# Attention decode with a feed-forward layer on one core: values in two contiguous halves, short weight rows over all partitions, a new order of work

## The chip, the cores and the metric

The kernel runs on one core of one Trainium2 chip. The core has a matrix engine (PE, whose weight loads are listed as PEld), a vector engine (DVE), a scalar engine (ACT), GpSimd (POOL) and a queue engine (SP) that issues the transfers from device memory; 16 DMA engines carry them out. The metric is the device time of one execution in microseconds (us), the median of three runs. Three runs of the kernel before took 311.46, 311.53 and 311.90 us.

## The reference

Four tokens (batch 4, sequence 1, width 448) go twice through the same attention layer and the same feed-forward layer. The attention has 16 query heads over 8 key/value heads of width 256, and looks at the last 2,048 of 8,192 cached positions.

```python
W = min(4096, max(256, Sk // 4))                  # 2048
q = (x @ wq) as [B, 16, 1, 256]
k, v = the last W rows of k_cache, v_cache, each head used by two query heads
p = softmax(q k^T * 256 ** -0.5);  o = p v
attention(x) = o @ wo
ffn(x) = (silu(x @ w_gate) * (x @ w_up)) @ w_down  # 448 -> 1792 -> 448

x = x + attention(layernorm(x));  x = x + ffn(layernorm(x))
x = x + attention(layernorm(x));  x = x + ffn(layernorm(x))
```

Both layers read the same caches. Keys and values of one token and one head are 1 MB each (2,048 x 256 in bf16). For 4 tokens and 8 heads that is 67 MB, and the second pass needs it all again. The weights are some 12 MB.

## The kernel before

**Work units.** One unit is a triple of token, layer and key/value head; there are 64. The tuple `PLAN` (line 64) orders them in 32 steps; each string holds groups, and a group is one unit or two joined with `+`. Its steps interleave tokens and layers: token 0 finishes layer 0 at step 4, token 1 at 12, token 2 at 18 and token 3 at 24 (counted from 0). When a token finishes a layer's heads, its output projection, norm and feed-forward and, for layer 0, its next query follow ("the crossing").

**Slots.** Keys and values come as halves of 512 KB into 27 slots of 128 partitions x 4 KB (`half`, line 355, `NPOOL`). `KEEP_K` and `KEEP_V` name how many heads of a token stay in their slots from layer 0 to layer 1; the rest are loaded twice. In all there are 90 key halves and 92 value halves.

**Loads.** A key half (line 817) takes, for each of the 128 partitions, 8 of that partition's 16 consecutive positions: one run of 4,096 bytes. A value half (line 830) takes two of four blocks of 512 positions; in each block a partition has 4 consecutive positions, so it receives two runs of 2,048 bytes. Weights load through `load` (line 495). Rows 384 to 447 of wq, w_gate and w_up are the last 64 of 448. They come as two DMAs each, one for each half of the columns, into partitions 0 to 63 and 64 to 127 (lines 503 and 515). All transfers are issued by SP in one queue.

**One group.** DVE transposes each key half in 32 x 32 blocks of 4-byte words (L822). POOL writes the masked query `qe` (L869). PE makes the scores: 32 matmuls for a group, over 8 slices of the width, two halves, and two parts (`scores1`, L852, for a group of one unit; `scores`, L864, for two). DVE takes maxima (L876, L890), PE spreads them (L881, L884), ACT takes the exponential into `praw` (L895, L898), with gaps between the written elements. PE turns the probabilities so that positions lie on partitions (`turn`, L912): two matmuls over 128 columns add up in the same place, one shifted against the other. ACT copies them out (L920), PE sums them (L928) and multiplies with the values (`pv`, L942, 8 matmuls for each half). DVE, POOL and PE normalise and flip the result (L933, L955, L959, L965, L975), and `out_proj` (L987, L995) adds the head's share of the output projection to a PSUM bank.

**The norm** (line 522) also makes `xe`, the last 64 features placed once in partitions 0 to 63 and once in 64 to 127 with zeros in the other half, as the two weight halves need them: one matmul (L540) and two DVE copies (L543, L545).

**What sets the order.** A planner (`Graph.schedule`, line 176) runs while the program is built. Each operation has an engine, an assumed duration and a rank; the planner walks through assumed time and gives each engine the ready operation of lowest rank. The resulting order is fixed, and each engine runs its list in order, with semaphore waits between engines. A load's rank follows from the unit's place (`KLEAD`, `KTAIL`, `VLAG`) plus an entry of the table `OFF` (line 47), which has 75 entries, for keys and values only. A load takes the slot that is free first. Idle stretches of PE on the assumed time are filled with matmuls on zeros (L1068, L1074). The crossing's operations have a rank 20 places lower than the unit that completes the token (`CROSS`).

The functions that the diff touches, and what calls them:

Of the kernel before, what the change touches and what calls it, by code (L numbers as in the profile page):

```python
# [25 lines left out]
NPOOL = 27  # L26
KEEP_K = (5, 5, 4, 5)
# [20 lines left out]
    ("k", 0, 0, 0): 1, ("k", 0, 0, 1): 2, ("k", 0, 0, 2): 0.5, ("k", 0, 0, 4): -8, ("k", 0, 1, 2): 0.5,  # L48
    ("k", 0, 1, 3): 1, ("k", 0, 1, 4): 4, ("k", 0, 1, 5): -1, ("k", 1, 0, 1): -3, ("k", 1, 0, 2): 1,
    ("k", 1, 0, 3): 1, ("k", 1, 0, 4): 0.5, ("k", 1, 0, 5): 0.5, ("k", 1, 0, 6): 1, ("k", 1, 0, 7): -0.5,  # L50
    ("k", 1, 1, 2): 1.5, ("k", 1, 1, 3): 1, ("k", 1, 1, 4): 1, ("k", 1, 1, 5): 2, ("k", 1, 1, 6): 2,
    ("k", 1, 1, 7): 2, ("k", 2, 0, 2): -1.5, ("k", 2, 0, 3): -2.5, ("k", 2, 0, 4): -2, ("k", 2, 0, 7): -0.5,
    ("k", 2, 1, 1): -2, ("k", 2, 1, 2): -2, ("k", 2, 1, 3): -4, ("k", 2, 1, 4): -2.5, ("k", 2, 1, 6): 2,
    ("k", 3, 0, 1): -0.5, ("k", 3, 0, 3): -0.5, ("k", 3, 0, 4): -2.5, ("k", 3, 0, 5): 1, ("k", 3, 0, 7): -0.5,
    ("k", 3, 1, 0): 1, ("k", 3, 1, 2): -1, ("k", 3, 1, 4): 5.5, ("k", 3, 1, 5): -0.5, ("k", 3, 1, 6): -2,
    ("k", 3, 1, 7): 0.5, ("v", 0, 0, 0): 0.5, ("v", 0, 0, 1): -3, ("v", 0, 0, 3): -3, ("v", 0, 0, 4): -7,
    ("v", 0, 0, 7): -2, ("v", 0, 1, 0): 0.5, ("v", 0, 1, 1): 0.5, ("v", 0, 1, 4): 0.5, ("v", 0, 1, 5): 0.5,
    ("v", 1, 0, 0): -0.5, ("v", 1, 0, 2): -2, ("v", 1, 0, 3): -1, ("v", 1, 0, 6): 1.5, ("v", 1, 1, 0): 1.5,
    ("v", 1, 1, 4): 2, ("v", 1, 1, 5): -1, ("v", 1, 1, 6): -1.5, ("v", 1, 1, 7): 2, ("v", 2, 0, 0): 1.5,
    ("v", 2, 0, 5): 0.5, ("v", 2, 0, 6): -0.5, ("v", 2, 1, 1): 1.5, ("v", 2, 1, 2): 1.5, ("v", 2, 1, 4): 0.5,  # L60
    ("v", 2, 1, 5): 6, ("v", 2, 1, 6): -3, ("v", 3, 0, 0): 2, ("v", 3, 0, 1): 3, ("v", 3, 0, 5): -0.5,
    ("v", 3, 1, 0): -0.5, ("v", 3, 1, 1): -3, ("v", 3, 1, 2): 4, ("v", 3, 1, 4): 2, ("v", 3, 1, 7): -2,
# [35 lines left out]
class Op:  # L98
    __slots__ = ("i", "eng", "dur", "rank", "emit", "deps", "succ", "nbytes", "dsem", "dval",
                 "start", "end", "pos", "waits", "inc", "val", "known", "run", "cell", "rel", "bank")  # L100

    def __init__(self, i, eng, dur, rank, emit):
        self.i, self.eng, self.dur, self.rank, self.emit = i, eng, dur, rank, emit
        self.deps = {}
        self.succ = []
        self.nbytes = 0
        self.dsem = None
        self.dval = 0
        self.cell = None
        self.rel = ()  # L110
        self.bank = ()
        self.inc = False
        self.val = 0
        self.waits = []


class Graph:
    filler = None

# [12 lines left out]
    def op(self, eng, dur, rank, emit, r=(), w=(), bank=(), acc=()):  # L132

        o = Op(len(self.ops), eng, dur, rank, emit)
        o.bank = bank
# [24 lines left out]
    def dma(self, rank, nbytes, emit, sem, r=(), w=(), run=8192, cell=None):  # L160

        o = self.op(SP, 0.05, rank, emit, r=r, w=w)
        o.run = run
        o.nbytes = nbytes
        o.cell = cell
        if cell is None:
            self._count(o, sem)
        return o
# [7 lines left out]
    def schedule(self, npool):  # L176
# [17 lines left out]
        while n < len(self.ops):  # L194
# [16 lines left out]
            if o.cell is not None:  # L211

                slot = min(pool)
                pool.remove(slot)
# [11 lines left out]
            avail[e].remove(o)  # L226
            o.start = t
# [114 lines left out]
def build(nc, A_x, A_k_cache, A_v_cache, A_wq, A_wo, B_x, B_w_gate, B_w_up, B_w_down, out):  # L342
# [3 lines left out]
    with ExitStack() as es:  # L346
# [8 lines left out]
        half = [sb(f"half{s}", [128, 8 * DH], BF16) for s in range(NPOOL)]  # L355
        identb = sb("identb", [128, 128], BF16)
        tiny = sb("tiny", [128, 14 + NS], BF16)
        onesb, qmask, osel, rsel = tiny[:, 0:1], tiny[:, 2:6], tiny[:, 6:10], tiny[:, 10:14]
        pmax = [tiny[:, 14 + s:15 + s] for s in range(NS)]
        tsel = sb("tsel", [128, 4, B], BF16)  # L360
        selt = [sb(f"selt{h}", [128, 4, 12], BF16) for h in range(2)]
        sel1 = [sb(f"sel1{h}", [128, 2, 4, 2, 2], BF16) for h in range(2)]
# [27 lines left out]
        praw = sb("praw", [128, 514], BF16)  # L390
# [28 lines left out]
        def c_fill(e):  # L419
# [7 lines left out]
            e.memset(xe[:, :, :], 0.0)  # L427
# [6 lines left out]
        g.op(DVE, 1.0, R0, c_fill, w=("onesf", "expo", "wrow", "qmask") + XE + XN +  # L434
# [7 lines left out]
        for h in range(2):  # L442
            g.op(DVE, 0.1, R0, lambda e, h=h: e.memset(selt[h][:, :, :], 0.0), w=(f"selt{h}",))
            for P in range(2):
                for y in range(2):
                    c0 = 8 * P + 2 * y
                    g.op(DVE, 0.1, R0, lambda e, h=h, P=P, c0=c0: e.tensor_copy(
                        selt[h][:, :, c0:c0 + 2], ivq[:, 2 * P + h, 0:4, :]), r=("identb",), w=(f"selt{h}",))
# [18 lines left out]
        ivt = identb[:, :].rearrange("p (h x z n) -> p h x z n", h=2, x=2, n=2)  # L467
        for h in range(2):
            for y in range(2):
                for x in range(2):  # L470
                    g.op(DVE, 0.1, R0, lambda e, h=h, y=y, x=x: e.tensor_copy(sel1[h][:, x, :, y, :], ivt[:, h, x, 0:4, :]),
                         r=("identb",), w=(f"sel1{h}{y}{x}",))
        for s_ in range(NS):
# [7 lines left out]
            rmask[:, :], idt.rearrange("p j t -> p t j"), AX.X, ALU.max), r=("identb",), w=("rmask",))  # L481
        iv = identb[:, :].rearrange("p (j z P y n) -> p j z P y n", j=4, P=2, y=2, n=2)
# [12 lines left out]
        def load(rank, nbytes, dst, src, key, run=8192):  # L495
            nw[0] += 1
            g.dma(rank, nbytes, lambda e: e.dma_start(dst, src), f"w{nw[0]}", w=key if isinstance(key, tuple) else (key,), run=run)  # L497

        load(-90, 4000, xio[0:B, :], A_x[:, 0, :], xio_k)
        for cc in range(3):  # L500
            load(-80, 1 << 20, wq_sb[:, 4096 * cc:4096 * (cc + 1)], A_wq[128 * cc:128 * cc + 128, :], f"wq{cc}")
        for h in range(2):
            load(-80, 1 << 18, wq_sb[64 * h:64 * h + 64, 3 * 4096:], A_wq[384:448, 2048 * h:2048 * h + 2048], f"wq3{h}", 4096)
        wo_v = A_wo.rearrange("(k p) n -> p k n", p=128)

        def load_wo(rank, kvh):
            load(rank, 458752, wo_sb[:, 4 * kvh:4 * kvh + 4, :].rearrange("p (h d) n -> p h (d n)", h=2),
                 A_wo[512 * kvh:512 * kvh + 512, :].rearrange("(h p d) n -> p h (d n)", h=2, d=2), f"wo{kvh}", 1792)

        def load_ffn(rank, rank_d):  # L510
            for nm, wsb, src in (("wg", wg_sb, B_w_gate), ("wu", wu_sb, B_w_up)):
                load(rank, 3 * 458752, wsb[:, 0:3 * FF].rearrange("p (c n) -> p c n", c=3),
                     src[0:384, :].rearrange("(c p) n -> p c n", p=128), nm + "a", 3584)
                for h in range(2):
                    load(rank, 114688, wsb[64 * h:64 * h + 64, 3 * FF:], src[384:448, 896 * h:896 * h + 896], f"{nm}b{h}", 1792)
            load(rank_d, 1605632, wd_sb[:, :, :], B_w_down.rearrange("(c p) n -> p c n", p=128), "wd", 896)
# [5 lines left out]
        def norm(t, rank, x):  # L522
# [17 lines left out]
            g.op(PE, 0.06, rank, lambda e: e.matmul(Z2[0:64, 16:17], lhsT=identb[:, 64:128], rhs=xn[:, 3, t:t + 1],  # L540
                                                    start=True, stop=True, skip_group_check=True),
                 r=(f"xn{t}", "identb"), w=("z2",), bank=("Z2",))
            vec(rank, lambda e: e.tensor_copy(xe[64:128, 1, t:t + 1], xn[64:128, 3, t:t + 1]), (f"xn{t}",),  # L543
                (f"xe{t}",), 0.08)
            vec(rank, lambda e: e.tensor_copy(xe[0:64, 0, t:t + 1], Z2[0:64, 16:17]), ("z2",), (f"xe{t}",), 0.1, ("Z2",))  # L545
# [23 lines left out]
        def qproj(ts, rank):  # L569
# [5 lines left out]
            for b, (zb, z, bank) in enumerate(banks):  # L575
# [13 lines left out]
                for c0, c1, rr, kw in ((0, 3, XN, dict(w=(z,))), (3, 4, XE, dict(acc=(z,)))):  # L589
                    g.op(PE, 0.43 * (c1 - c0), rank, lambda e, zb=zb, b=b, c0=c0, c1=c1: q_mm(e, zb, b, c0, c1),  # L590
                         r=rr + tuple(f"wq{c}" for c in ((0, 1, 2) if c0 == 0 else (30, 31))), bank=(bank,), **kw)
# [34 lines left out]
        def ffn_row(ts, rank):  # L626
# [24 lines left out]
            for gi, (z, bank, w) in enumerate((("z", "Z", "wg"), ("z2", "Z2", "wu"))):  # L651
                g.op(PE, 1.28, rank, lambda e, gi=gi: gu(e, gi, 0, 3), r=XN + (w + "a",), w=(z,), bank=(bank,))
                g.op(PE, 0.5, rank, lambda e, gi=gi: gu(e, gi, 3, 4), r=XE + (w + "b0", w + "b1"), acc=(z,), bank=(bank,))
# [491 lines left out]
```

## Time and profile before

| | |
|---|---|
| three runs | 311.46, 311.53, 311.90 us |
| the profiled execution's own time | the page gives its span, 309.8 us, and no other |
| PE, DVE, ACT, POOL busy | 78%, 65%, 23%, 28% of the span |
| read from device memory | 107.58 MB, 347 GB/s over the span |
| hardware DMA queue | 93.3% of the 16 engines' span |
| value halves, key halves | 92 and 90 of 512 KB |
| key transposes on DVE (L822) | 90, 1,234 ns each, 110.5 us in all |

A line of the windows view gives a stretch and its length, the busy time and the number of instructions of each engine, the clock granted to PE, the busy share of the DMA engines (a little over 1 is possible, since packets overlap) and the rate. The chain of waits goes back from the last instruction: at each step to what released it, or to the instruction before it on its engine. SPq is time in SP's queue, "issue" is time in which an engine waited for nothing that the profile shows. The clock is given in parts of full speed.

### The profile page before, as it was taken

What the parts mean: (1) busy time and instruction counts of PE and PEld (TensorE: products, weight loads), DVE (VectorE), ACT (ScalarE), POOL (GpSimd) and SP (SyncE); (2) the same over time, 40 slices, a digit from 0 to 9 for tenths busy, and PEclk for the clock granted to TensorE, in tenths of its full rate; (3) what the DMA queues carried; (4) which work ended last, traced back from release to release, by engine and by line L of the source; (5) the groups of instructions that cost most, each with busy time, mean ns of one, the idle gap of its engine ahead of it and who ended that gap; (6) DMA issues with size and microseconds to landing.
All of it is one profiled execution on the core that took longest, in us unless ns stands there. A gap on an engine that the chain in (4) does not pass through costs nothing.

```text
span 309.8 us, 11390 instructions
## 1 busy us (share of the span) xinstructions
PE 240.2 (78%) x4972; PEld 136.9 (44%) x4972; DVE 202.1 (65%) x641; ACT 70.0 (23%) x203; POOL 88.3 (28%) x233
## 2 busy tenths in 40 slices
PE   0578686776779787799788798788988787986976
PEld 0323224334234444454345545564554446554554
DVE  8534377746254887978587878682689679375542
ACT  0030003131104232313132223211422320231410
POOL 1511102222103233322325332412324322244330
PEclk9999759796577897956787777655857955596975
DMA  7999999999999999999999999999899999899200
GB/s 265 333 383 399 389 403 403 393 394 351 332 394 391 392 394 399 376 381 375 373 369 380 399 397 399 393 395 351 310 382 401 396 393 401 297 324 390 85 3 3
DMA packets 43746, 108.33 MB, mean 350 GB/s; under 512 B 3240, under 2 KB 7344, under 8 KB 43312
## 3 DMA queue, kind: packets, MB, share of 16 engines
q1 hardware_dynamic: 43696, 107.60, 93.3%
q8 instruction: 39, 0.64, 0.9%
q14 instruction: 11, 0.09, 0.1%
HBM read 107.58 MB, written 0.00 MB: 347 GB/s over the span
## 4 chain that ended last, share of the span: by engine, by line
DMA 35%; PE 32%; SPq 15%; DVE 11%; issue 5%; ACT 1%; DVEq 0%
DMA half<-in_A_k_cache_dram 20%; DMA half<-in_A_v_cache_dram 13%; PE Y L942 8%; DVE half L822 6%; SPq L830 5%; SPq L817 5%; PE S L852 5%; SPq L497 4%; PE Z L586 4%; PE Z L702 2%; DVE oh L959 2%; DMA wg_sb<-in_B_w_gate_dram 2%; PE Z L729 2%; PE A L995 1%; PE Z L532 1%
## 5 line engine op out<-in xcount | busy, mean ns | idle before, releaser
L822 DVE STREAM_TRANSPOSE half<-half 128x1024 uint32<-128x1024 uint32 x90 | 110.5, 1234 | 23.6 <-DMA half<-in_A_k_cache_dram 23.3
L955 POOL TENSOR_TENSOR small<-small 128x2 f32<-128x2 f32 (+1 forms) x58 | 42.5, 735 | 81.1 <-DVE small L933 79.4
L942 PE MATMUL Y<-half,pT 128*4 128x256 bf16 (+1 forms) x1024 | 55.1, 324 | 12.2 <-DMA half<-in_A_v_cache_dram 6.9
L852 PE MATMUL S<-half,qe 128*8 128x128 bf16 x1664 | 41.6, 251 | 5.0 <-DVE half L822 2.3
L869 POOL TENSOR_TENSOR qe<-qc,tiny 128x64 bf16<-128x64 bf16 x64 | 18.3, 294 | 77.1 <-PE S L852 47.0
L957 ACT ACTIVATE oh<-Y 128x256 bf16<-128x256 f32 x58 | 22.2, 384 | 72.9 <-PE Y L942 67.5
L898 ACT ACTIVATE praw<-S,small 104x128 bf16<-104x128 f32 x52 | 19.1, 367 | 67.7 <-DVE small L890 67.3
L852 PEld LDWEIGHTS S<-half,qe 128*8 128x8 bf16 x1664 | 29.6, 95 | 10.1 <-DVE half L822 3.8
L959 DVE SCALAR_TENSOR_TENSOR oh<-oh,small,Y 128x256 bf16<-128x256 bf16 x58 | 27.0, 465 | 10.0 <-ACT oh L957 8.9
L942 PEld LDWEIGHTS Y<-half,pT 128*4 128x4 bf16 (+1 forms) x1024 | 20.1, 89 | 24.6 <-DMA half<-in_A_v_cache_dram 12.1
L876 DVE TENSOR_REDUCE tiny<-S 104x1 bf16<-104x128 f32 (+1 forms) x58 | 16.9, 294 | 9.2 <-PE S L852 9.0
L920 ACT ACTIVATE pT<-Y 128x64 bf16<-128x64 f32 (+1 forms) x58 | 13.6, 234 | 27.8 <-PE Y L912 27.5
L1068 PE MATMUL A<-identb,small 128*128 128x512 bf16 x48 | 19.8, 528 | 0.0
L881 PE MATMUL S<-small,identb 104*104 104x32 bf16 x58 | 12.8, 229 | 7.3 <-DVE tiny L876 5.5
L995 PE MATMUL A<-wo_sb,oT 128*4 128x448 bf16 x148 | 15.1, 405 | 2.9 <-DVE oT L975 2.6
L933 DVE TENSOR_REDUCE small<-Y 128x2 f32<-128x32 f32 (+1 forms) x58 | 10.4, 183 | 10.6 <-PE Y L928 10.4
L532 PE MATMUL Z<-st,small 128*128 128x2 f32 x32 | 9.0, 350 | 9.9 <-DVE st L529 9.0
L912 PE MATMUL Y<-sel,praw 104*128 104x32 bf16 x208 | 14.1, 184 | 3.3 <-ACT praw L898 2.8
L965 PE MATMUL Y<-tiny,oh 128*128 128x2 bf16 (+1 forms) x116 | 11.8, 171 | 6.1 <-DVE oh L959 5.3
L975 DVE TENSOR_TENSOR oT<-Y,small 128x4 bf16<-128x4 f32 (+1 forms) x62 | 9.2, 154 | 9.1 <-PE Y L965 8.4
L965 PEld LDWEIGHTS Y<-tiny,oh 128*128 128x128 bf16 x116 | 6.9, 101 | 18.1 <-DVE oh L959 12.9
L586 PE MATMUL Z<-wq_sb,xn 128*4 128x512 bf16 x120 | 14.1, 601 | 0.3 <-DVE st L538 0.3
(137 smaller groups left out, 302.1 us busy)
## 6 DMA issues: line engine op xcount, KB each, us to landing
half<-in_A_v_cache_dram SPq DMA_DIRECT2D x92, 512.0 KB, 9.4
half<-in_A_k_cache_dram SPq DMA_DIRECT2D x90, 512.0 KB, 8.8
wo_sb<-in_A_wo_dram SPq DMA_DIRECT2D x8, 448.0 KB, 13.5
wq_sb<-in_A_wq_dram SPq DMA_DIRECT2D x3, 1024.0 KB, 7.0
wd_sb<-in_B_w_down_dram SPq DMA_DIRECT2D x1, 1568.0 KB, 17.6
wg_sb<-in_B_w_gate_dram SPq DMA_DIRECT2D x1, 1344.0 KB, 15.5
wu_sb<-in_B_w_up_dram SPq DMA_DIRECT2D x1, 1344.0 KB, 16.8
wq_sb<-in_A_wq_dram SPq DMA_DIRECT2D x2, 256.0 KB, 11.6
```

The lines of the kernel that those rows point to most:

```text
L586: last = e.matmul(zb[32 * j:32 * j + B, 0:512], lhsT=lhsT, rhs=wq_sb[:, c:c + 512], start=(cc == 0), stop=(cc == 3), skip_group_check=True)
L822: return e.transpose(a, a)
L852: last = e.matmul(Sb[s_][qd:qd + 8, 0:128], lhsT=qe[q_][:, 0, ce, :, :].rearrange("p a n -> p (a n)"), rhs=kt[:, ce // 2, ce % 2, 2 * x:2 ...
L869: g.op(POOL, 0.25, pos - SLEAD - 1, lambda e, P=P, t=t, kvh=kvh: e.tensor_tensor(qe[q_][:, P, :, :, :], qc[t][:, kvh, :, :].unsqueeze(2).b ...
L898: return e.activation(praw[0:R, 2:258].rearrange("p (g r h l) -> p h g r l", g=2, h=2, l=2)[:, 0, :, :, :], Sb[s_][0:R, 0:128].rearrange(" ...
L942: last = e.matmul(Yb[p_][32 * gg:32 * gg + M, 256:512], lhsT=pT[pt][:, gg, 2 * hv + a, 4 * P:4 * P + M] if n == 2 else p1[:, gg % 2, gg // ...
L955: g.op(POOL, 0.69, pos, lambda e: e.tensor_tensor(ri[p_][:, 0:2 * n], rs[p_][:, 0:2 * n], expo[:, 1:1 + 2 * n], op=ALU.pow), r=(f"rs{p_}", ...
L957: g.op(SCA, 0.34, pos, lambda e: e.activation(oh[:, :], Yb[p_][:, 256:512], ACT.Copy), r=(f"y{p_}",), w=("oh",), bank=(f"Y{p_}",))
L959: g.op(DVE, 0.43, pos, lambda e: e.scalar_tensor_tensor(out=oh[:, :], in0=oh[:, :], scalar=lomask[:, 0:1], in1=Yb[p_][:, 256:512], op0=ALU ...
L965: last = e.matmul(Yb[p_][:, 2 * n * dh:2 * n * dh + 2 * n], lhsT=oh[:, :].rearrange("p (m e) -> p e m", e=2)[:, dh, :], rhs=osel[:, 0:2 * ...
L995: last = e.matmul(Ab[32 * k:32 * k + B, 0:D], lhsT=oT[oi][:, k % 2, k // 2, :], rhs=wo_sb[:, 4 * kvh + k, :], start=False, stop=False, ski ...
L1068: return e.matmul(Ab[:, 0:512], lhsT=zero[:, 0:1].broadcast_to([128, 128]), rhs=identb[:, :].unsqueeze(1).broadcast_to([128, 4, 128]), sta ...
```

## The change

**Values.** The 2,048 positions are cut into two contiguous halves of 1,024. In a half each partition has 8 consecutive positions: one run of 4,096 bytes. With that the positions' places on partitions and in score columns change. A group's score matmul now takes its columns from both key halves at once (`keys`): with one access over two slots, if the slots are at most `REACH` = 15 apart, otherwise with two matmuls of half the width. Whichever of the two key slots is lower holds the first half (`which`). All slots are one tensor for this (`kv`). The planner gives the second key half a free slot near the first (`mate`) and adds 0.35 us to the assumed duration of a pair that is far apart (`FAR_DUR`).

**Turn.** The exponential is written without gaps, and `turn` writes its two results to partitions 0 to 63 and 64 to 127 from 64 columns each, instead of adding two results over 128.

**Last 64 rows.** wq, w_gate and w_up each get one DMA for them: row r goes to partitions 2r and 2r + 1, half of the columns each. `xe` follows: a matmul with `twice` copies each of the 64 features to two partitions, and one DVE multiplication with `par` keeps the right one.

**Order.** `OFF` has 198 entries, for keys (k), values (v), weights (w), groups (g), transposes (t), output projections (o) and crossings (d), and applies to the operations of all engines by a tag. The run lengths that the planner assumes for weights are lower (wq 2000, wo 950, gate and up 800 and 950, down 430).

```diff
 NPOOL = 27
+HALF = 8 * DH
+REACH = 15
+FAR_DUR = 0.35
...
 OFF = {
-    ("k", 0, 0, 0): 1, ("k", 0, 0, 1): 2, ("k", 0, 0, 2): 0.5, ("k", 0, 0, 4): -8, ("k", 0, 1, 2): 0.5,
...
+    ("d", 4): -7, ("d", 12): -6.5, ("d", 18): -7, ("d", 21): 0.5, ("d", 24): -6.5, ("d", 27): -0.5, ("d", 31): 2,
+    ("g", 0, 0, 1): -8, ("g", 0, 0, 3): 4.5, ("g", 0, 0, 4): -7, ("g", 0, 0, 5): -1, ("g", 0, 0, 6): -3,
...
+    ("v", 3, 1, 6): 1.5, ("w", 1): 7, ("w", 2): -8, ("w", 3): 0.5, ("w", 4): 8, ("w", 5): 6, ("w", 7): -4,
...
-        o = Op(len(self.ops), eng, dur, rank, emit)
-        o.bank = bank
+        o = Op(len(self.ops), eng, dur, rank + OFF.get(self.tag, 0.0), emit)
+        o.bank, o.tag = bank, self.tag
...
                 slot = min(pool)
+                if o.mate:
+                    near = [s for s in pool if s[0] <= t + 1e-9 and abs(s[1] - o.mate[0]) <= REACH]
+                    slot = min(near) if near else slot
...
+            o.dur += FAR_DUR * sum(abs(a[0] - b[0]) > REACH for a, b in o.pairs)
...
-        half = [sb(f"half{s}", [128, 8 * DH], BF16) for s in range(NPOOL)]
+        kv = sb("half", [128, NPOOL * HALF], BF16)
...
-        for h in range(2):
-            load(-80, 1 << 18, wq_sb[64 * h:64 * h + 64, 3 * 4096:], A_wq[384:448, 2048 * h:2048 * h + 2048], f"wq3{h}", 4096)
+        load(-80, 1 << 19, wq_sb[:, 3 * 4096:], A_wq[384:448, :].rearrange("r (h c) -> (r h) c", h=2), "wq3", 4096)
...
-                for h in range(2):
-                    load(rank, 114688, wsb[64 * h:64 * h + 64, 3 * FF:], src[384:448, 896 * h:896 * h + 896], f"{nm}b{h}", 1792)
+                load(rank, 229376, wsb[:, 3 * FF:], src[384:448, :].rearrange("r (h c) -> (r h) c", h=2), nm + "b", 950)
...
-            vec(rank, lambda e: e.tensor_copy(xe[64:128, 1, t:t + 1], xn[64:128, 3, t:t + 1]), (f"xn{t}",),
-                (f"xe{t}",), 0.08)
-            vec(rank, lambda e: e.tensor_copy(xe[0:64, 0, t:t + 1], Z2[0:64, 16:17]), ("z2",), (f"xe{t}",), 0.1, ("Z2",))
+            g.op(PE, 0.06, rank, lambda e: e.matmul(Z2[:, 16:17], lhsT=twice[:, :],
+                                                    rhs=xn[:, 3, t:t + 1], start=True, stop=True, skip_group_check=True),
+                 r=(f"xn{t}", "twice"), w=("z2",), bank=("Z2",))
+            vec(rank, lambda e: e.tensor_tensor(xe[:, :, t], par[:, :], Z2[:, 16:17].broadcast_to([128, 2]), op=ALU.mult),
+                ("z2", "par"), (f"xe{t}",), 0.14, ("Z2",))
...
+        def which(cell, kc):
+            return int(cell[0] == max(kc[0][0], kc[1][0]))
+
+        def keys(kc, j, nj, ce):
+            lo, hi = sorted((kc[0][0], kc[1][0]))
+            at = [kv[:, HALF * c + 256 * j + 64 * (ce // 2) + ce % 2:] for c in (lo, hi)]
+            if hi - lo <= REACH:
+                return [(0, bass.AP(at[0].tensor, at[0].offset, [list(at[0].ap[0]), [HALF * (hi - lo), 2], [256, nj], [2, 32]]))]
+            return [(32 * nj * i, bass.AP(v.tensor, v.offset, [list(v.ap[0]), [256, nj], [2, 32]])) for i, v in enumerate(at)]
...
-                    vsrc = A_v_cache[t, kvh, s0:s0 + WIN, :].rearrange("(a q g) d -> q a g d", a=4, q=128)
+                    vsrc = A_v_cache[t, kvh, s0:s0 + WIN, :].rearrange("(a q g) d -> a q (g d)", a=2, q=128)
...
-                            half[cell[0]][:, :].rearrange("p (a g d) -> p a g d", a=2, g=4),
-                            vsrc[:, 2 * hv:2 * hv + 2, :, :]), None, w=(f"v{t}_{kvh}_{hv}",), run=2048, cell=cell)
+                            unit(cell), vsrc[hv]), None, w=(f"v{t}_{kvh}_{hv}",), run=4096, cell=cell)
...
+                    for x in range(X):
                         for P in range(n):
-                            kt = half[kcs[P][hf][0]][:, :].rearrange("p (j c r v) -> p c v j r", j=8, c=4, v=2)
-                            qd = 64 * P + 32 * hf
...
+                            qd = 64 * P + 32 * x
+                            for i, (c0, rhs) in enumerate(keys(kcs[P], J * x, J, ce)):
+                                last = e.matmul(Sb[s_][qd:qd + 8, c0:c0 + rhs.free_size()],
+                                                lhsT=qe[q_][:, P, ce, :, :].rearrange("p a n -> p (a n)"), rhs=rhs,
+                                                start=(ce == 0 and i == 0), stop=(ce == 7), skip_group_check=True)
...
-                        last = e.matmul(o, lhsT=praw[0:R, c0:c0 + 128], rhs=w,
-                                        start=(gg == 0 and h == 0), stop=False, skip_group_check=True)
+                        last = e.matmul(Yb[p_][64 * h:64 * h + 64, c0:c0 + (48 if n == 2 else 32)],
+                                        lhsT=praw[0:R, 64 * gg:64 * gg + 64], rhs=w,
+                                        start=(gg == 0), stop=False, skip_group_check=True)
```

## The prediction

> **What bounds the kernel now.** I read part 2 of the page first: for each fortieth of the span (7.75 us), how busy the 16 DMA engines were and what they moved.
>
> ```profile
> DMA  7999999999999999999999999999899999899200
> GB/s 265 333 383 399 389 403 403 393 394 351 332 394 391 392 394 399 376 381 375 373 369 380 399 397 399 393 395 351 310 382 401 396 393 401 297 324 390 85 3 3
> ```
>
> The engines are full from the second slice to the 37th, about 288 us of 309.8. The rate is not constant: dips at slices 2, 10 to 11, 28 to 29 and 35 to 36, most of them at full occupancy. A shorter transfer stream therefore shortens the kernel, unless the engines behind it cannot follow. Next come windows with something special in them (columns: window, length, PE, PEld, DVE, ACT, POOL, clock, DMA share, GB/s).
>
> ```profile
> 254.00:258.90 4.90, 4.30 (x81) 2.71 (x80) 3.90 (x14) 0.38 (x1) 1.77 (x6) 0.50 1.03 406
> 62.50:66.50 4.00, 2.96 (x79) 1.64 (x79) 1.71 (x8) 0.87 (x3) 1.26 (x3) 1.00 1.05 387
> 10.50:14.00 3.50, 2.50 (x9) 1.79 (x9) 1.27 (x9) 0.00 (x0) 2.89 (x9) 1.00 1.03 245
> 73.00:83.00 10.00, 6.63 (x93) 3.49 (x96) 3.44 (x14) 1.28 (x3) 2.70 (x8) 0.50 1.05 308
> ```
>
> The first holds only keys, the second only values, the third the end of wq's third block and its last rows in two 64-partition loads, the fourth gate and up with theirs. All run at share 1.03 to 1.05; the rate falls to 245 and 308. The packet counts of the first and of the second:
>
> ```profile
> DMA packets 543, 1.99 MB, mean 406 GB/s; under 512 B 60, under 2 KB 60, under 8 KB 542
> ...
> q1 hardware_dynamic: 542, 1.97, 101.3%
> ```
>
> ```profile
> DMA packets 795, 1.55 MB, mean 387 GB/s; under 512 B 47, under 2 KB 47, under 8 KB 794
> ...
> q1 hardware_dynamic: 794, 1.53, 103.7%
> ```
>
> Without the small ones these are 482 packets of 4,096 B and 747 of 2,048 B, so the windows are pure. Keys: 1.97 MB / 4.9 us = 402 GB/s. Values: 1.53 / 4.0 = 382 GB/s. Last, the chain of waits by engine, and its pieces where the last token changes layer:
>
> ```profile
> DMA 35%; PE 32%; SPq 15%; DVE 11%; issue 5%; ACT 1%; DVEq 0%
> ```
>
> ```profile
> 239.97 11.65 DMA half<-in_A_v_cache_dram
> 251.62 0.04 issue
> 251.66 0.60 PE Y L942 x6
> ...
> 256.50 0.15 DVE st L543
> ...
> 273.70 6.91 DMA half<-in_A_k_cache_dram
> 280.60 0.02 issue
> 280.63 0.03 DVE half L822
> ```
>
> DMA and SP's queue are half the chain. Until 251.6 it comes back to a landing; then follow 22 us of token 3's crossing (output projection, norm, feed-forward, next query), a load issued into a freed slot, and compute to 309.8.
>
> **The change part by part.**
>
> *Value runs.* 92 value halves are 48.23 MB. At 382 GB/s they take 126.1 us, at the keys' 402 they take 120.0: 6.1 us less, 0.066 us a half. The new shape, values in one contiguous 512 KB, is not in the trace. Its lower bound is 0 (the rate belongs to the source and not to the run); its upper bound is the 419 GB/s of the windows view from 4.5 to 9.5 us, where wq comes in 8 KB runs: 126.1 - 115.1 = 11.0. I take 6.1, since run and destination are then exactly the keys'. The Trainium skill, "DMA: Bandwidth & Descriptors", section Specifications, gives 512 B as the least transfer for line rate. By that rule 2 KB and 4 KB runs are equal, this term is 0 and the time would be 308.2; the two windows above, 5% apart with full engines, speak against it.
>
> *Last rows of wq.* From 10.5 to 14.0 us the engines move 0.86 MB. At 402 GB/s this takes 2.1 us, so 1.4 is saved. Bounds: 0 (slow for another reason) and 1.4.
>
> *Last rows of gate and up.* 73 to 83 us moves 3.08 MB in 10.0 us. At the 382 GB/s of the stretch 83 to 84 us, which is only w_down's short packets, it takes 8.1: 1.9 saved. Bounds: 0, and 2.3 at 402.
>
> The stream is 6.1 + 1.4 + 1.9 = 9.4 us shorter. Three DMAs fewer (some 0.6 us of issue each) save nothing: SP is ahead there.
>
> *What reaches the end.* The loads have no inputs, so SP's order follows their ranks. By the sorted ranks, the last value half of token 3, layer 0 has 76 value halves and 93.95 MB up to and with itself in both, and 26 halves behind it. So up to the chain's 251.6 the stream gives 76 x 0.066 + 1.4 + 1.9 = 8.3. After it the chain is compute plus one load queued for 6.9 us behind others, two or three of them values: 0.2 more. From 203 to 237 the compute is late and not the stream (DMA share 0.99 against 1.03, clock 0.61); some 13 value halves land there, and their 0.9 is lost. On the path: 8.3 + 0.2 - 0.9 = 7.6.
>
> *Order fitted anew.* 198 offsets in place of 75, now for all engines. The unknown is two-sided. Gain: at most the starved part, where the share is below the usual 1.04: (1.04 - 0.88) x 8 in 216 to 224 and again in 264 to 272, and about 1.6 in the neighbouring 8 us windows: 4.2 us. Loss: the nearest row is one head's work put ahead of the crossing, two key transposes of 1.2, scores of 0.95, values of two times 0.55: 4.5 us. The ranks speak for neither end. The crossing's own work goes 6.5 earlier (the entry for plan step 24), the loads keep their places. I take 0.
>
> *Scores over two cells.* The same 32 matmuls of the same width for a group whose cells are at most 15 apart; else 64 of half the width. Nearest row: 32 of them hold PE for 0.95 us. Bounds: 0, and 58 x 0.95 = 55 us of PE time, a third of it on the chain, 18 us. Of the 351 pairs of 27 slots 66 are further apart than 15, 19%, and the slot choice now prefers near ones; I take 3 of 58, about 1 us on the path, and set it against the next part.
>
> *Smaller edits.* The turn's matmuls (L912, 184 ns) fill 64 columns instead of 128, and two can stand side by side; exp writes without gaps. Each is between 0 and 0.05 us per group; with 58 groups and a third on the path at most 1 us gained. The norm loses one copy: the chain shows 0.15 for it (L543). These cancel the far pairs. Set-up on DVE loses four copies and a memset and gains two operations; all lie under the wait for wq (landing at about 15 us). Token input x now sits behind 1 MB of wq in SP's queue, some 2.5 us later; DVE's set-up, which runs until 9 us, hides it, and without that cover it would cost those 2.5 us.
>
> **Sum.** 309.8 - 7.6 = 302.2 for the span. The page gives no other time for this execution; the runs' median 311.53 is 1.7 above the span, so I add 1.7: 303.9.
>
> **The rivals.**
>
> *Compute catches up.* The engines that follow the stream become the bound. For it: half of the chain is PE, DVE, ACT and issue, and DVE is over 90% busy in the page's fullest slices. Against it: until 251.6 the chain keeps coming back to landings. If only half of the 8.3 passes: 311.5 - 4.2 = 307.3.
>
> *Runs do not matter.* Value transfers are slow for their source, not for 2 KB: only 1.4 + 1.9 remain, 308.2. For it: the source pattern changes too. Against: the source was already two contiguous blocks.
>
> *The 64-partition loads are innocent,* the dips having another cause: 7.6 - 3.3 = 4.3, so 307.2. Against: both dips stand exactly where such loads are in flight.
>
> *The fit closes the starved stretches:* 303.9 - 4.2 = 299.7.
>
> *Slower: the crossing of token 3 gets longer.* PE and DVE run in order, and every other head's work put ahead of the crossing costs 4.5 us at a place with no cover (251.7 to 273.7). Two heads, 9.0, exceed the 7.6 gained: 312.9. One does not decide. For it: 34 transposes and 47 groups have new ranks, up to 8 places. Against: the crossing itself moves earlier by 6.5.
>
> **How the numbers follow.** Forecast (301 to 306.5) 0.56, starved stretches closed 0.10, compute catches up 0.14, runs do not matter 0.05, 64-partition loads innocent 0.03: faster 0.88. Longer crossing 0.10: slower. Between them, 0.02: same. A difference under 0.2% (0.6 us) can't be told from none. The range reaches from the closed stretches (299.7) to where runs do not matter (308.2, and 0.3 for the rounding of the rates): it leaves out the slower tenth, the 0.02, and what lies beyond its ends.
>
> **What would show it.** Value-only windows near 402 GB/s with 4,096 B packets; no 2,048 B packets at all; no dip to 245 near 12 us, and gate and up at over 370 GB/s; the stream's end near 281 instead of 289 us and about 20 us of compute after it. Wrong steps show as: values still at 382; DMA shares below 1.0 in more windows (compute caught up); or a longer stretch between the last value landing of token 3, layer 0 and its next query. The prediction is wrong above all if the new order starves the stream more often than the old.

## The result and the profile after

The changed kernel takes 300.88 us, the median of five runs from 298.74 to 307.12; the kernel before takes 311.53 beside it. The ratio is 0.9632, with a 95% interval of 0.9566 to 0.9698: 11.5 us less (9.4 to 13.5), where the forecast was 303.9, or 7.6 less. Here and below, ratio and interval go by the faster executions alone (307.12 is not among them), so that a gain worked out from them is not quite the difference of the two medians, which is 10.7 us here. The profiled execution took 302.74 us, of which the span is 300.8.

Parts 2 and 3 of the changed kernel's page (fortieths of the span, 7.5 us each):

```profile
DMA  7999999999999999999998999999999997999100
GB/s 283 404 400 406 409 406 404 399 406 403 395 408 404 399 409 383 362 403 382 372 401 321 418 409 405 409 407 394 351 402 410 407 408 302 334 311 417 57 2 3
DMA packets 31921, 108.32 MB, mean 360 GB/s; under 512 B 3192, under 2 KB 7296, under 8 KB 31488
...
q1 hardware_dynamic: 31872, 107.60, 91.8%
```

The dips at slices 2 and 10 to 11 (333, 351, 332 GB/s) are gone: there now stand 404, 403 and 395. Those near the end have moved, not gone: 321 in slice 22, 351 in slice 29, 302 to 334 in slices 34 to 36. But the new order has also moved the loads that stood there. The short rows of wq land at 9.4 us (15.0 before), ahead of its third block, and those of up and gate at 51.9 and 52.5 (82.8 and 77.5 before), some 25 and 19 us ahead of their large loads. Five windows (columns: window, length, PE, PEld, DVE, ACT, POOL, clock, DMA share, GB/s): the former places of the dips, the new places of the short rows, and a stretch of values alone:

```profile
10.50:14.00 3.50, 2.61 (x10) 1.77 (x11) 0.93 (x7) 0.00 (x0) 2.96 (x9) 1.00 0.97 387
70.00:80.00 10.00, 8.42 (x154) 4.97 (x142) 6.61 (x22) 1.81 (x5) 2.49 (x10) 0.64 1.05 395
8.00:9.50 1.50, 0.44 (x2) 0.44 (x2) 1.43 (x19) 0.00 (x0) 0.00 (x0) 1.00 1.06 442
50.00:53.00 3.00, 2.52 (x26) 1.07 (x25) 0.58 (x3) 0.00 (x0) 0.99 (x2) 1.00 1.05 406
84.20:87.20 3.00, 2.42 (x65) 1.55 (x69) 2.49 (x13) 0.00 (x0) 0.23 (x1) 1.00 1.03 410
```

387 stands where there were 245, and 395 where there were 308, but no short rows are in flight there any more. That they no longer slow the stream is seen at their new places, 442 and 406 GB/s, beside e4_changed_split below. The DMA view of the last window:

```profile
DMA packets 340, 1.23 MB, mean 410 GB/s; under 512 B 40, under 2 KB 40, under 8 KB 340
...
q1 hardware_dynamic: 340, 1.23, 102.7%
```

Without the 40 small packets these are 300 of 4,096 B, 1.23 MB. Values move at 410 GB/s; 402 was forecast and 382 was the rate of two runs of 2,048 B. In the whole trace there is no packet of 2,048 B; before there were 23,552. Last, the chain of waits by engine, and its pieces in order of time (start, length, what) near the end:

```profile
DMA 50%; PE 25%; DVE 13%; SPq 9%; issue 2%; ACT 1%; POOL 1%
```

```profile
243.87 9.59 DMA half<-in_A_k_cache_dram
...
257.99 7.19 DMA half<-in_A_k_cache_dram
...
268.09 11.48 DMA half<-in_A_v_cache_dram
279.57 0.04 issue
279.61 0.60 PE Y L982 x8
```

DMA's share of the chain was 35% before; in a second profiled execution of the changed kernel (a1_changed below) it is 38%, so the 50% are not to be leaned on. Before, the chain was compute alone from 251.6 to 273.7. Now landings interrupt that stretch twice. The last load lands at 282.0 (290.0 before) and 18.8 us follow it (19.8 before); in a1_changed it lands at 280.1 and 20.7 follow.

### The profile page after: what moved, and what is told of

The parts are those of the page before. It is cut to its first block, busy times and chain, and to the rows that moved or that the text cites. A ratio compares the mean times of both kernels' runs of the same rounds, so it can differ in the third digit from the quotient of the medians.

```text
span 300.8 us, 11298 instructions
## 1 busy us (share of the span) xinstructions
PE 237.5 (79%) x4946; PEld 137.7 (46%) x4946; DVE 200.8 (67%) x622; ACT 69.2 (23%) x203; POOL 88.2 (29%) x233
## 4 chain that ended last, share of the span: by engine, by line
DMA 50%; PE 25%; DVE 13%; SPq 9%; issue 2%; ACT 1%; POOL 1%
DMA half<-in_A_k_cache_dram 27%; DMA half<-in_A_v_cache_dram 23%; DVE half L873 8%; PE Y L982 7%; PE S L907 6%; SPq L868 4%; SPq L536 3%; SPq L883 2%; PE A L1035 2%; PE Z L739 2%; PE Y L951 1%; PE Z L685 1%; PE S L925 1%; DVE oh L999 1%; PE Z L570 1%
## 5 line engine op out<-in xcount | busy, mean ns | idle before, releaser
L982 PE MATMUL Y<-half,pT 128*4 128x256 bf16 (+1 forms) x1024 | 56.8, 338 | 18.2 <-DMA half<-in_A_v_cache_dram 14.7
L907 PE MATMUL S<-half,qe 128*8 128x128 bf16 (+1 forms) x1856 | 52.7, 269 | 7.4 <-DVE half L873 3.3
L907 PEld LDWEIGHTS S<-half,qe 128*8 128x8 bf16 x1856 | 36.6, 100 | 15.5 <-DVE half L873 5.3
L938 ACT ACTIVATE praw<-S,small 104x128 bf16<-104x128 f32 (+1 forms) x58 | 21.8, 377 | 72.3 <-DVE small L934 64.5
L982 PEld LDWEIGHTS Y<-half,pT 128*4 128x4 bf16 (+1 forms) x1024 | 19.4, 90 | 32.6 <-DMA half<-in_A_v_cache_dram 20.3
L960 ACT ACTIVATE pT<-Y 128x64 bf16<-128x64 f32 (+1 forms) x58 | 13.5, 233 | 37.8 <-PE Y L951 31.8
L934 DVE TENSOR_REDUCE small<-S 104x1 f32<-104x32 f32 x58 | 10.3, 180 | 10.8 <-PE S L928 5.7
L1113 PE MATMUL A<-identb,small 128*128 128x512 bf16 x46 | 16.9, 468 | 0.0
L925 PE MATMUL S<-small,identb 104*104 104x32 bf16 x58 | 13.7, 237 | 3.7 <-DVE tiny L920 3.0
L951 PE MATMUL Y<-sel,praw 104*64 104x32 bf16 x208 | 13.5, 205 | 1.9 <-DVE oT L1015 1.2
L925 PEld LDWEIGHTS S<-small,identb 104*104 104x104 bf16 x58 | 8.2, 141 | 14.2 <-DVE tiny L920 7.5
(134 smaller groups left out, 273.7 us busy)
## 6 DMA issues: line engine op xcount, KB each, us to landing
wo_sb<-in_A_wo_dram SPq DMA_DIRECT2D x8, 448.0 KB, 13.5
```

Source lines behind the costliest of these rows:

```text
L907: last = e.matmul(Sb[s_][qd:qd + 8, c0:c0 + rhs.free_size()], lhsT=qe[q_][:, P, ce, :, :].rearrange("p a n -> p (a n)"), rhs=rhs, start=(c ...
L925: e.matmul(Sb[s_][0:R, 256:288], lhsT=identb[0:R, 0:R], rhs=far[0:R, :, :, :].broadcast_to([R, 2, 8, 2]) if n == 2 else far1[0:R, :, :].br ...
L938: return e.activation(praw[0:R, 0:128 * n].rearrange("p (g r l) -> p g r l", g=2 * n, l=2), Sb[s_][0:R, 0:128 * n].rearrange("p (l g r) -> ...
L982: last = e.matmul(Yb[p_][32 * gg:32 * gg + M, 256:512], lhsT=pT[pt][:, gg, 2 * a + hv, 4 * P:4 * P + M] if n == 2 else p1[:, gg % 2, 2 * a ...
L1113: return e.matmul(Ab[:, 0:512], lhsT=zero[:, 0:1].broadcast_to([128, 128]), rhs=identb[:, :].unsqueeze(1).broadcast_to([128, 4, 128]), sta ...
```

## The experiments

All are timed in five rounds against the kernel before on the same chip, whose medians there were 312.79, 312.15 and 312.33 us. "Gain" is one minus the ratio, times that median, with its interval. Landing times are read from the traces, each of one execution. "The 76th half" is the 76th value half that SP issues, with 26 halves behind it: the load that lands at 251.6 us before, with which the forecast reckoned.

**One part alone, in the order of before.** First the value runs:

```diff
-rearrange("(a q g) d -> q a g d", a=4, q=128)
+rearrange("(a q g) d -> a q (g d)", a=2, q=128)
-half[cell[0]][:, :].rearrange("p (a g d) -> p a g d", a=2, g=4), vsrc[:, 2 * hv:2 * hv + 2, :, :]
+half[cell[0]][:, :], vsrc[hv]
```

> The kernel before with one edit: each value half is one contiguous block of 1,024 positions, 4,096 bytes per partition, instead of two blocks with 2,048. Every engine's order stays that of before. The probabilities still belong to the old places, so values are weighted with the wrong positions' probabilities; the work is the same. The theory of the prediction (transfer 6.1 us shorter, 0.9 of it lost where compute is late): 306.3 us, value windows at 402 GB/s. Rival 'runs do not matter': 311.5, windows at 382. Rival 'compute catches up': half of 6.1 passes, 308.5, with windows at 402 and more starved stretches. Theory 'the transfers were priced too low' (the 3 us by which the changed kernel beat the sum come from here): 304 or less.

Measured: 308.01 us, ratio 0.9859 (0.9802 to 0.9915), a gain of 4.4 (2.7 to 6.2). The forecast for this run was 306.3, and 308.5 if compute catches up by half; the interval holds both. Values alone, in the window of before:

```profile
62.50:66.50 4.00, 3.33 (x86) 1.55 (x75) 1.28 (x6) 1.05 (x4) 0.99 (x2) 1.00 1.03 406
...
DMA packets 440, 1.62 MB, mean 406 GB/s; under 512 B 47, under 2 KB 47, under 8 KB 439
...
q1 hardware_dynamic: 439, 1.61, 100.8%
```

Without the 47 small packets these are 392 of 4,096 B: 1.61 MB / 4.0 us = 401 GB/s, where 382 stood. Runs of 4 KB in place of 2 KB are worth something by themselves. The edit also makes each half one contiguous block at its source; that this is not needed is argued from the keys, whose 4 KB runs have gaps between them and moved at 402. The last load lands 3.4 us earlier (286.65), less than the 6.1 priced for the transfers, and the 76th half 2.3 earlier, less than the 5.0 less 0.9 priced for it. Windows of this kernel show where some went:

```profile
96.00:104.00 8.00, 6.65 (x197) 3.98 (x198) 6.56 (x16) 2.54 (x8) 2.31 (x8) 0.93 0.90 324
208.00:216.00 8.00, 7.37 (x98) 3.09 (x89) 1.10 (x7) 1.99 (x4) 2.03 (x5) 0.50 0.90 335
264.00:272.00 8.00, 7.64 (x139) 3.65 (x139) 3.88 (x16) 2.73 (x7) 3.83 (x10) 0.80 0.85 266
```

The DMA shares are 0.90, 0.90 and 0.85, and were 1.01, 0.99 and 0.88 before. Over the 33 windows of 8 us from 16 to 280 us, those under 1.0 fall short of the usual 1.04 by 4.6 us before (six windows) and by 7.4 here (nine). So the engines run dry for longer once the values come faster, which is part of what compute catching up would look like.

Then the short rows, with one DMA over 128 partitions each and all else as before:

```diff
-for h in range(2): load(-80, 1 << 18, wq_sb[64*h:64*h+64, 3*4096:], A_wq[384:448, 2048*h:2048*h+2048], ...)
+load(-80, 1 << 19, wq_sb[:, 3*4096:], A_wq[384:448, :].rearrange("r (h c) -> (r h) c", h=2), ("wq30", "wq31"), 4096)
-for h in range(2): load(rank, 114688, wsb[64*h:64*h+64, 3*FF:], src[384:448, 896*h:896*h+896], ...)
+load(rank, 229376, wsb[:, 3*FF:], src[384:448, :].rearrange("r (h c) -> (r h) c", h=2), (nm+"b0", nm+"b1"), 1792)
```

> The kernel before with the last 64 rows of wq, gate and up in one DMA each over 128 partitions, and nothing else; all other instructions and their order are those of before. The multiplier xe is left as it was, so these rows meet the wrong features; the work is the same. The theory of the prediction (1.4 + 1.9 us of the stream): 308.2 us, no dip to 245 GB/s near 12 us, gate and up over 370 GB/s. Rival '64-partition loads innocent': 311.5 with the same dips. If the transfers were priced too low: 307 or less.

Measured: 307.47 us, ratio 0.9834 (0.9784 to 0.9885), a gain of 5.2 (3.6 to 6.8). Its windows, at the very times of the dips:

```profile
10.50:14.00 3.50, 2.51 (x9) 1.79 (x9) 1.25 (x9) 0.00 (x0) 2.90 (x9) 1.00 1.02 414
73.00:83.00 10.00, 9.21 (x99) 3.73 (x94) 2.94 (x10) 1.28 (x3) 2.59 (x7) 0.55 1.05 392
```

245 and 308 became 414 and 392, so the pairs of 64-partition loads made the dips. In the first window a packet of 4,096 B took 288 ns before and 159 ns here (medians). Why is open: whether the number of partitions does it or the number of loads was not separated. The last rows of wq land 1.9 us earlier (15.0 to 13.1), w_down 4.2 earlier (86.7 to 82.5), the 76th half 3.3 earlier: 3.3 was priced for wq, gate and up together. This execution's span is 3.3 shorter as well. The interval of the median's 5.2 begins at 3.6, and no view located more than 4.2.

Both together:

> Both edits together on the kernel before (4,096-byte value runs; last 64 rows in one DMA each), with the order and all compute of before; probabilities and features meet the wrong positions as in the single edits. The theory of the prediction puts the whole gain here: 311.5 - 7.6 = 303.9, and the 3 us more of the changed kernel then belong to its new order. If the transfers were priced too low: about 301. If compute catches up: 307. If the two edits add up, the gain is the sum of the single ones.

Measured: 303.40 us, ratio 0.9707 (0.9653 to 0.976), a gain of 9.2 (7.5 to 10.9); 4.4 and 5.2 make 9.6. The parts add up within their intervals. The forecast for the two was 7.6, which the interval just holds. The 76th half lands 7.8 earlier (243.9), where the forecast had 8.3 less 0.9.

**The changed kernel, unedited and with the transfers put back.**

> The changed kernel itself, unedited, so that it stands on one chip with the three runs that undo parts of it. Expected: 0.963 of the time before, as first measured; 0.958 to 0.970.

Measured: 302.44 us, ratio 0.9645 (0.9583 to 0.9707), a gain of 11.1. The runs spread from 298.21 to 304.04.

```diff
-unit(cell), vsrc[hv]
+unit(cell).rearrange("p (a g d) -> p a g d", a=2, g=4), vsrc[:, 2 * hv:2 * hv + 2, :, :]
```

> The changed kernel with 2,048-byte value runs again (two blocks of 512 positions in each half); every engine's order is that of the changed kernel, and values meet probabilities of other positions. In the old order this part was worth 4.4 to 4.8 us. If it is worth the same in the new order: 4 to 5 us above the changed kernel. If the new order leaves less compute that is late (the prediction's 0.9 comes back, and nothing else is lost): 6.1 above. If compute is the bound in the new order: less than 3.

Measured: 305.39 us, ratio 0.978 (0.9716 to 0.9844). Beside a1_changed the short runs cost 0.0135, 4.2 us (1.4 to 7.0 from the two intervals).

```diff
-load(-80, 1 << 19, wq_sb[:, 3*4096:], A_wq[384:448, :].rearrange(...), "wq3", 4096)
+load(-80, 1 << 18, wq_sb[0:64, 3*4096:], A_wq[384:448, 0:2048], "wq3", 4096)
+more(-80, 1 << 18, wq_sb[64:128, 3*4096:], A_wq[384:448, 2048:4096], "wq3x", 4096)
...
```

(The dots stand for the same edit on gate and up; `more` issues a second DMA under the same tag.)

> The changed kernel with the last 64 rows of wq, gate and up in two 64-partition DMAs each again; every engine's order is that of the changed kernel (SP issues three more), and these rows meet the wrong features. Alone in the old order this was worth 5.2 us by the times and 4.2 us by the landings. The prediction priced it at 3.3. In the new order the small gate and up loads are issued earlier, apart from the large ones, so they slow value and key loads instead: 3 to 5 us above the changed kernel. If the price came from their meeting the large gate and up loads: 1.5 to 2.5 above.

Measured: 306.19 us, ratio 0.9774 (0.9714 to 0.9833): the 64-partition loads cost 0.0129, 4.0 us (1.3 to 6.7). The windows of the short rows' new places in this kernel, against 442 and 406 in the changed one:

```profile
8.00:9.50 1.50, 0.43 (x2) 0.44 (x2) 1.43 (x19) 0.00 (x0) 0.00 (x0) 1.00 1.10 259
50.00:53.00 3.00, 2.72 (x67) 1.55 (x60) 0.58 (x3) 0.22 (x2) 0.99 (x2) 1.00 1.06 250
```

The dips come back where these loads now stand. With both edits at once only the new order, the layout of positions and the turn are left of the change:

> The changed kernel with both transfers as before: 2,048-byte value runs and 64-partition loads; what is left of the change is the new order, the score layout and the turn, with the misplacements of the single edits. If the order term is 0, as predicted: the time before, 1.00 of it. If the order gives the 2.3 us that separate the changed kernel (0.963) from both transfer edits in the old order (0.971): 0.992. If the new order only pays with the faster transfers: at or above 1.00.

Measured: 309.31 us, ratio 0.9927 (0.9888 to 0.9967), a gain of 2.3 (1.0 to 3.5). What the forecast put at nothing is a small gain. Landings show when it arises: w_down 0.9 us earlier, the 76th half 2.5 earlier, the last load 2.7 earlier, and the end 0.4 closer to it. The starved windows did not close, they moved: this kernel's shares in 216 to 224 and 264 to 272 are 0.96 and 1.00 (0.88 and 0.88 before), but 256 to 264 holds 0.80 (1.03 before). By the count used above the shortfall is 3.9 us in place of 4.6, so the new order by itself does not starve the stream more than the old one. Which of order, layout and turn gives the 2.3 wasn't separated.

**The old table in the new layout.** `OFF` of before, everything else as changed:

> The changed kernel with the table of offsets of before (75 entries, keys and values alone); loads, score layout, turn and the planner's new assumed run lengths stay as changed. It computes the reference. If a fitted table is worth nothing by itself (the order term 0 of the prediction): about 304, as with both edits in the old order. If the table only fits the planner it was fitted with: slower than 304, between 305 and 312, with more starved windows (DMA share under 1.0 while the stream runs), and the new table is then needed to keep the gain. If the offsets' effect is the 3 us of surplus: 304.

Measured: 315.58 us, ratio 1.009 (1.0056 to 1.0123), some 14 us above the changed kernel and also above the 305 to 312 expected if the table fits only its planner. The GB/s row of its page, and the waits of SP's queue from 110 to 170 us (total, times, longest; L845 issues key halves here):

```profile
GB/s 273 392 398 405 406 409 405 408 406 390 407 394 393 410 388 241 301 320 317 330 404 343 352 416 402 402 405 303 329 355 412 406 407 407 251 260 401 87 4 3
```

```profile
SPq L845 <- PE Y L945: 13.8, 2, 10.0
```

From slice 16 to 20 the stream starves at 241 to 330 GB/s: SP waited for slots, once for 10 us. This is not the order of before. The planner's assumed durations and slot choice have changed, and from the same table it makes another order, in which 7 of 58 groups have key slots too far apart (their score matmuls count 2,080 in place of 1,856). So the run doesn't price the old order, which only the kernels made from the one before keep. It shows that the new layout and planner with this table lose more than the transfers gain.

**What far slots cost.** In the changed kernel the score row has 1,856 matmuls, 58 times 32: no group is far apart. The split form for all 58, the planner's order kept:

```diff
-            if hi - lo <= REACH:
+            if hi < lo:
```

> The changed kernel with the split access for all 58 score groups: 64 matmuls of half the width instead of 32, as for a pair of slots far apart, and nothing else changed or reordered; it computes the reference. The prediction bounded this at 55 us of PE time and 18 us on the path (0.33 us a group), 0 at the other end. By that: 0.9645 of before plus 18 us, 1.02. If PE has room beside the stream: under 0.98. The trace shows what 64 half-width matmuls hold PE for (0.95 us for 32 now, 1.9 if their number sets it, 0.95 if their width does).

Measured: 343.21 us, ratio 1.0975 (1.0924 to 1.1027), 41.5 us above the changed kernel's 0.9645: 0.72 us for each group on average. A small part of it is PE time: all score matmuls of this kernel together, then those of the changed one (busy us, mean ns, idle time before them and what ended it):

```profile
L907 PE MATMUL S<-half,qe 128*8 128x64 bf16 (+1 forms) x3712 | 61.1, 229 | 33.7 <-issue 28.3
L907 PE MATMUL S<-half,qe 128*8 128x128 bf16 (+1 forms) x1856 | 52.7, 269 | 7.4 <-DVE half L873 3.3
```

61.1 us are 8.4 more than 52.7, and 11.1 more than the 50.0 of a1_changed. On the chain a group of 64 matmuls often takes 0.97 us, about the 0.95 of 32. The pieces of the chain, with what follows:

```profile
105.79 0.97 PE S L907 x64
...
110.47 0.95 PE S L907 x58
111.41 3.42 issue
114.83 0.29 PE S L907 x6
...
126.28 3.24 issue
```

PE stops in the middle of a group and waits for nothing that the profile names. Parts 3 and 4 of its page:

```profile
q8 instruction: 53, 0.87, 1.0%
...
PE 52%; issue 16%; DMA 14%; DVE 9%; SPq 7%; ACT 2%
```

The unedited kernel has 39 of these instruction packets of 16 KB; its chain has "issue" at 5% in a1_changed and at 2% in the execution shown first. The 16 issue pieces over 1 us on this chain add up to 43.2 us; the chain of a1_changed has four, 8.4 us, and the other has none. Each of the 16 ends 1.3 to 1.6 us after one of the instruction packets has landed. Some of them (times in us, from the trace; the last column counts the matmuls, weight loads, semaphore and drain instructions of PE that started before the stop, of 13,666 in all):

```
PE stops   packet landed   PE goes on   after the packet   instructions before
 48.10         50.09          51.38          1.29                  961
 99.55        102.10         103.49          1.39                 2753
111.41        113.51         114.83          1.32                 3265
126.28        128.14         129.52          1.38                 4033
193.18        195.26         196.76          1.50                 7105
242.53        244.60         246.13          1.53                 9409
303.54        306.07         307.48          1.41                12225
```

All 16 counts leave the same remainder, 193, when divided by 256, and so do those of the six such stops of PE in a1_changed. Stops of this kind come only at this one place in every 256 instructions, and last until shortly after a packet has landed: PE is waiting for its own instructions. How much of the 41.5 us this costs is less certain: the stops on the chain are 34.8 us more than in a1_changed and 43.2 more than in the other execution of the unedited kernel, PE is busy for 251.5 us in place of 231.5 (a1_changed), and no kernel altered the fetching alone. Why the packets come late is open too. The Trainium skill, "Runtime: NRT & Kernel Launch", section Instruction fetch mechanics, says that instructions come in blocks of 16 KiB, 256 instructions, and that this is hidden behind the time to issue them. The first half agrees, by the remainders, and by the number of packets to within a block: 53 x 256 = 13,568, and the trace has 13,604 of PE's matmuls and weight loads; 39 x 256 = 9,984 against 9,892. The second half does not hold in this run, by its 16 stops.

**Fillers and the clock.** The matmuls on zeros were left out (`FILL0 = 1000`), or made all 128 columns wide instead of small ones after 62 us (`FILLB = 1000`):

> The changed kernel without the 64 filling matmuls on zeros (46 of 128 columns are in the trace as L1113, the rest as quarters); everything else and its order are unchanged. It asks whether the granted clock of PE is a part of the gain that the sum left out. If the clock sets the compute stretches: mean clock clearly below 0.75 and the time 3 us or more above the changed kernel (0.9645 of before, so 0.974 or more). If fillers only take PE time: 0.955 to 0.963. If the stream sets the time and PE follows either way: 0.961 to 0.968.

> The changed kernel with every filling matmul over all 128 columns, also after 62 us of the planner's time, where four over 32 columns stand otherwise; everything else is unchanged. If the clock answers to how much of the array is busy: mean clock above 0.79 and 2 us or more off the changed kernel's time (0.958 of before or less). If the clock does not matter for the time: 0.961 to 0.968.

Measured: 301.25 us (ratio 0.9644, 0.9603 to 0.9684) and 301.36 us (0.9644, 0.9594 to 0.9695). Span and mean granted clock of the kernel without fillers, then of the unedited one:

```profile
core 0: 298.8 us, clock 0.686
```

```profile
core 0: 300.8 us, clock 0.786
```

These are the two profiled executions; over the six runs of each the mean is 0.70 without fillers and 0.76 with them (a1_changed), and the ratio is the same to within some 2 us of interval. So fillers neither gain nor cost more than that here, and a mean clock lower by 0.06 did not lengthen the time. With wider fillers the mean was 0.77 and not above 0.79, the condition of its expectation, so that run says nothing of a higher clock. Neither explains why runs of the changed kernel spread over 6 us, which stays open. No kernel tried is faster than the changed one beyond the intervals.

## Why the prediction was right, and where its sum was off

The time lies in the stated range, at 300.9 just below the 301 to 306.5 of the forecast itself. The mechanism, a shorter transfer stream that reaches the end, was right; the sum was 3.9 us short (11.5 by the ratio against 7.6).

*Value runs.* The rate went from 382 to 401 GB/s in e2_before_4k and to 410 in the changed kernel; 402 was forecast. Of the forecast's 6.1 us of transfers, 4.3 were put on the path (76 halves at 0.066, and 0.2, less 0.9); the edit alone gave 4.4 and taking it out of the changed kernel cost 4.2. The step held in size, but so close a match is luck: the first interval reaches from 2.7 to 6.2, and the landings of that execution show only 2.3 and 3.4. It cannot tell whether the discount for late compute was right. That runs do not matter is refuted by e2_before_4k, and with it, for these transfers, the 512 B of the Trainium skill, "DMA: Bandwidth & Descriptors", section Specifications.

*Short rows.* Forecast 3.3, measured 5.2 (3.6 to 6.8) alone and 4.0 in the new order. The mechanism was right: that the 64-partition loads are innocent is refuted by e3_before_rows, whose dips go while all else stands. The size was low. The priced windows at the rates that e3_before_rows reached give 0.86 MB at 414, 1.4 us, and 3.08 MB at 392, 2.1: 3.5. Between these 3.5, the landings' 3.3 to 4.2 and the median's 5.2 no view decides.

*Order fitted anew.* This is the term that was off most: taken as 0 between -4.2 and +4.5, measured 2.3 less (1.0 to 3.5, layout and turn included). The two together account for the miss: 9.2 for the transfers and 2.3 for the rest make 11.5, which is what was measured, against 7.6. That it agrees to a tenth is luck, since each of the three has an interval of 1 to 2 us to either side.

*Scores over two cells.* Three far groups of 58 were assumed; there are none. And the upper bound was wrong: 18 us for all 58, worked out as PE time with a third of it on the chain, where the run shows 41.5. The nearest row was near the PE time (0.95 us a group; 61.1 us in all 58, 1.05 each) but blind to the number of instructions. At the average of 0.72 us three groups would have cost 2.2 us, not 1, if the cost is even, which no run shows.

*Rivals.* Compute did not catch up by half: the transfers alone brought 9.2, more than the whole 7.6. It does lag more at the end, as the forecast's sign for it would show: the DMA share from 252 to 274 us is 0.88, against 0.97 before. The crossing of token 3 did not become longer: from the landing of the 76th half to the first matmul of the next query it takes 15.4 us, 16.8 before. The starved stretches did not close, and the time came to lie between that rival's 299.7 and the forecast all the same.

*Signs.* 4,096 B packets in value windows, none of 2,048 B, the stream's end at 282.0 (281 forecast) and 18.8 us of compute after it (20) came as written. No dip near 12 us and gate and up above 370 GB/s came too, but the short rows are no longer there, so these two signs show little; 442 and 406 at the new places show it. One sign of a wrong step came as well: by the count above the changed kernel has nine windows under a share of 1.0 in place of six, and a shortfall of 7.7 us in place of 4.6. The order by itself is not its cause, by e7_changed_neither's 3.9; with the transfers alone, e6_before_both, it is 6.7. So the faster stream finds the engines behind it late more often, as the rival of late compute says, but it costs far less than that rival's half.

## What to carry to other kernels

Where transfer engines are full and the rate still dips, look at which load is in flight at the dip: two 64-partition loads held a whole stretch at 245 GB/s, and 128-partition loads of the same bytes in place of three such pairs gave some 4 to 5 us back. Price an edit that doubles a short instruction by the count of instructions too, not by its engine time alone. A table of offsets fitted to one layout is no baseline in another; to price the parts of a change, put them into the kernel whose order they leave alone. And when an order changes, look where a load now stands before reading its old window.

## What the runs showed of the hardware

PE can run out of instructions: with 13,604 matmuls and weight loads in place of 9,892 it stopped 16 times for 1.3 to 3.9 us, each time at the same place in a block of 256 instructions and until 1.3 to 1.6 us after a 16 KB instruction packet had landed. The profile lists such a stop as "issue". The changed kernel has a few of them as well (2.7 us at 275.85 in a1_changed), though its other profiled execution has none over 1 us and the same span. And a full load stream on this one core held 399 to 418 GB/s in 25 of the first 37 slices of the changed kernel.
